# The last pass of a two-layer attention and MLP backward: the first dV chunk put ahead of delta, and dW operands in four row strips

## The chip, the cores and the metric

The kernel runs on one core of a Trainium2 chip. The metric is device time in microseconds of one execution, the median of several runs; lower is better. A profiled execution of the kernel before is read besides.

## The reference

Two residual layers, an attention block (A) and an MLP block (B), are applied twice with the same weights, to two tokens (batch 2, one position each). The outputs are the result and the gradients of nine inputs for a given `grad_out`. Cut to what matters:

```python
q = (x @ wq).reshape(B, 1, 32, 128)              # D = 1024, 32 query heads, 4 kv heads
scores = einsum("bhqd,bhkd->bhqk", q, k) * 128 ** -0.5   # 16384 cached keys
p = softmax(scores); o = einsum("bhqk,bhkd->bhqd", p, v)
A = o.reshape(B, 1, 4096) @ wo
B = gelu(layernorm(x) @ w1 + b1) @ w2 + b2       # F = 3584
x = x + A(layernorm(x)); x = x + B(layernorm(x)) # twice
grads = vjp(f)(grad_out)                         # dx, dK, dV, dWq, dWo, dW1, db1, dW2, db2
```

All tensors are bf16. K and V are 32 MB each, and so are dK and dV, which sum over both layers.

## The kernel before

Vectors live as columns: 128 partitions by (128-blocks x 2 tokens). Work runs in passes: layer 0 and layer 1 forward, then backward through layer 1, the second MLP, layer 0. A weight or cache tile (128 x 4096 bf16, 1 MB) comes in by SP's DMA queue; PE transposes its 128x128 blocks against an identity, ACT or DVE copies the result out of PSUM, and PE multiplies. Exponentials of both layers stay on chip (`e_all`).

**Evacuations.** `evac_bf16` (lines 150 to 156) and `evac_cast` (158 to 164) copy out of PSUM on ACT or on DVE, whichever has the smaller running cost in `load`; `only["e"] = "A"` forces ACT. The program order on each engine is the order of emission (a manual schedule).

**Before the last pass.** The backward of Wo for layer 0 is `wob`, an `Ahead`: its 32 row blocks are loaded and transposed in place by `wob.row` while the gradient is not yet there; every fifth (`dotted`: 4, 9, ... 29) is not transposed but done by DVE dot products (`wob.dots`, line 337). `wob.products` (line 379) makes dO. `do_delta` scales dO by the softmax's reciprocal sums (`dof`, 837 and 841), casts it to `doT_bf`, multiplies by o, sums over partitions on PE (`part_sum`, line 182) and writes the negated sums (delta) as three bf16 parts into `dlr` (849 to 861).

**The last pass** makes dV and dK of both layers at once, dQ of layer 0, and all weight gradients. A group `g` is one (batch, kv head); `order` runs through eight groups, each in four chunks of 4096 keys; `chunks[i]` is the i-th of the 32. For a chunk: `make_blks` (1197) transposes its coefficients (for dV: `e_all`; for dK: `dX`) into `blk`; `make_qm` (1165 to 1173) spreads the columns of dO or q into `Qm`; `kv_pair(w, i, h)` (1222) makes half a chunk of dV or dK with 8 matmuls into four PSUM banks and four copies, and after the second half stores the chunk (POOL's queue, line 1045). `scores` (1257) multiplies V by dO, `ds0` (1261, 1265) subtracts delta by a product with `dlr` and multiplies by `e_all` into `dX`; `dq_quad` (450) multiplies K by `dX`.

The first group is kept on chip (`keepV0` to `keepV3`, `keepK0` to `keepK3`) and is done ahead of the main loop: per chunk scores, `ds0`, and one `kv_pair`. Then the loop over steps `m` begins; a step takes two 8-block slices of V through transposes (line 1367), `scores`, at most one chunk's `make_blks`, `kv_pair`s, and with `step_fill` 1 unit (first four steps) or 5 units of weight-gradient work.

**Weight-gradient units.** dW = xT y over only four rows (two layers x two tokens). `rows_unit` (1012) transposes column vectors into rows: one source per 32-partition strip of `rowsA` and `rowsB`. A dW unit (1081) is one matmul, 4 x 128 by 4 x 512, into one of four banks and one copy; each weight gradient keeps to one strip (dW2 strip 0, dW1 strip 1, dWo strip 2, dWq strip 3). `fill` alternates dW2 and dW1 units, then dWo; `late` holds dWq of a kv head whose dq is done.

**Tiles and queues.** Staging tiles and load tiles are the same set: `new_home` takes a free tile for a store, `load_tile` one for a load (stored ones first, so the load waits for the store to land). `pump` issues loads while at most `NLD` are open and more than `spare` tiles are free. SP's queue and POOL's run in order. What the page calls L163 and L160 are the copies of `evac_cast`, L155 and L152 those of `evac_bf16`.

Of the kernel before, what the change touches and what calls it, by code (L numbers as in the profile page):

```python
# [9 lines left out]
BF16 = mybir.dt.bfloat16  # L10
# [13 lines left out]
def kernel(  # L24
# [155 lines left out]
    def part_sum(src, n, name):  # L180
        ps = pm_([128, n], F32, name)
        PE.matmul(ps[:], lhsT=onesf[:], rhs=src, start=True, stop=True)
        return ps
# [157 lines left out]
    class Ahead:  # L341


        def __init__(self, W, n_in, name, xT_bf=None, fps=None):
            self.W, self.J, self.x, self.fps, self.name = W, n_in // 128, xT_bf, fps, name
            self.dotted = range(4, self.J, 5)
            self.dp = vec.tile([128, len(self.dotted), 2], F32, name=name + "_dp")
            self.chunks = list(w_chunks(n_in, D))
            self.rows = {}
# [379 lines left out]
    n_all = vec.tile([128, DJ, 4], BF16, name="n_all")  # L729
    o_all = vec.tile([128, HQ, 4], BF16, name="o_all")  # L730
    dq_all = vec.tile([128, HQ, 4], BF16, name="dq_all")
    gA_all = vec.tile([128, DJ, 4], BF16, name="gA_all")
    m_all = vec.tile([128, DJ, 4], BF16, name="m_all")
    h_all = vec.tile([128, FJ, 4], BF16, name="h_all")
    dh_all = vec.tile([128, FJ, 4], BF16, name="dh_all")
    gM_all = vec.tile([128, DJ, 4], BF16, name="gM_all")
# [91 lines left out]
    def attn_out_bwd(l, gT):  # L828
        V.tensor_copy(out=gA_all[:, :, lsl(l)], in_=gT[:])
        _, dops = w_pass(A_wo, HD, D, "do_ps", gT_bf=gA_all[:, :, lsl(l)])  # L830
        return do_delta(l, dops)

    def do_delta(l, dops, ahead=None):
        sv = saved[f"a{l}"]
        dof = wrk.tile([128, G, 8], F32, name="dof")
        for b in range(2):
            V.tensor_tensor(out=dof[:, b * HKV:(b + 1) * HKV, :].rearrange("p k r -> p (k r)"), in0=dops[:, :, b],
                            in1=sv["rbc"][:, b * HKV:(b + 1) * HKV, :].rearrange("p k r -> p (k r)"), op=ALU.mult)
            if ahead is not None:
                r_ = sv["rbc"][:, b * HKV:(b + 1) * HKV, :].rearrange("p k r -> p (k r)")  # L840
                V.tensor_tensor(out=dof[:, b * HKV:(b + 1) * HKV, :].rearrange("p k r -> p (k r)")[:, 4:HQ:5],
                                in0=ahead.dp[:, :, b], in1=r_[:, 4:HQ:5], op=ALU.mult)
        doT_bf = vec.tile([128, G, 8], BF16, name=f"doT_bf{l}")
        V.tensor_copy(out=doT_bf[:], in_=dof[:])
        prod = wrk.tile([128, G, 8], F32, name="dprod")
        V.tensor_tensor(out=prod[:], in0=dof[:], in1=sv["oT"][:], op=ALU.mult)
        dlp = part_sum(prod[:].rearrange("p g r -> p (g r)"), G * 8, "dl_ps")
        rest_ = wrk.tile([128, G * 8], F32, name="dl_rest")
        V.tensor_scalar(out=rest_[:], in0=dlp[:], scalar1=-1.0, scalar2=None, op0=ALU.mult)
# [12 lines left out]
        saved[f"a{l}"]["doT_bf"] = doT_bf  # L862
        return doT_bf
# [94 lines left out]
    x4 = mlp_out(1, fps[:, 0:DJ * WIDE].rearrange("p (j b) -> p j b", b=WIDE)[:, :, 0:2])  # L958
    sv = saved["m0"]
# [33 lines left out]
    TP = [pt([128, 8, 128], BF16, "tpm%d" % i) for i in range(2)]  # L993
    for t in TP:
        V.memset(t[:].bitcast(F32), 0.0)
    do_delta(0, pairs(dops, HQ), wob)

    rowsA = ld.tile([128, LDW], BF16, name="rowsA", tag="ld")  # L1000
    rowsB = wrk.tile([128, D], BF16, name="rowsB", tag="rowout")

    def rows_unit(srcs, dst, j0):

        def u():
            tp = mtp()
            n = 0
            for i, (colT, jlo) in srcs.items():
                jn = min(8, colT.shape[1] - jlo)
                n = max(n, jn)  # L1010
                for j in range(jn):
                    PE.transpose(tp[32 * i:32 * i + 4, j, :], colT[:, jlo + j, :], ident[:], tile_position=(0, 32 * i))  # L1012
            lo, hi = 32 * min(srcs), 32 * max(srcs) + 4
            evac_bf16(dst[lo:hi, j0 * 128:(j0 + n) * 128], tp[lo:hi, 0:n, :].rearrange("p a b -> p (a b)"), n * 128)

        return Unit(u)

    X = [px([128, 512], F32, "xm%d" % i) for i in range(4)]
    rot = {"x": 0, "tp": 0}


    by_read = deque(ld.tile([128, LDW], BF16, name="big", tag="ld") for _ in range(NLD - 1))
    by_store = deque()

    def nxt(what, lst):
        rot[what] += 1
        return lst[(rot[what] - 1) % len(lst)]

    def mx():
        return nxt("x", X)  # L1030

    def mtp():
        return nxt("tp", TP)

    def n_free():
        return len(by_read) + len(by_store)

    def new_home():
        return (by_read or by_store).popleft()

    def load_tile():
        return (by_store or by_read).popleft()

    def store(out_ap, view, tile_):
        nc.gpsimd.dma_start(out_ap, view)  # L1045
        by_store.append(tile_)

    class Unit:
        def __init__(self, f, home=False):
            self.f, self.home = f, home  # L1050

        def ready(self):
            return not self.home or n_free() > 3

        def __call__(self):
            self.f()

    def dbias(rows, i, n, out_ap, name):
        p = 32 * i
        row = new_home()  # L1060
        for c0 in range(0, n, 512):
            ps = mx()
            PE.matmul(ps[p:p + 1, :], lhsT=ones_bf[p:p + 4, 0:1], rhs=rows[p:p + 4, c0:c0 + 512], start=True, stop=True,
                      tile_position=(p, p))
            evac_cast(row[p:p + 1, c0:c0 + 512], ps[p:p + 1, :], 512)
        store(out_ap.rearrange("(o f) -> o f", o=1), row[p:p + 1, 0:n], row)

    def dw_units(xrows, yrows, i, chunks, y0, ny, out_of):

        p = 32 * i  # L1070
        box = {}
        units = []
        for j0, rb in chunks:
            for j in range(rb):
                for c0 in range(0, ny, 512):
                    def u(j0=j0, rb=rb, j=j, c0=c0):
                        if j == 0 and c0 == 0:
                            box["t"] = new_home()
                        sv_ = box["t"][:, 0:rb * ny].rearrange("p (j n) -> p j n", j=rb)
                        ps = mx()  # L1080
                        PE.matmul(ps[:], lhsT=xrows[p:p + 4, (j0 + j) * 128:(j0 + j + 1) * 128],  # L1081
                                  rhs=yrows[p:p + 4, y0 + c0:y0 + c0 + 512], start=True, stop=True, tile_position=(p, 0))
                        evac_cast(sv_[:, j, c0:c0 + 512], ps[:], 512)
                        if j == rb - 1 and c0 + 512 >= ny:
                            store(out_of(j0, rb), sv_, box["t"])
                    units.append(Unit(u, j == 0 and c0 == 0))
        return units

    def rows_of(out_ap):
        return lambda j0, rb: out_ap[j0 * 128:(j0 + rb) * 128, :].rearrange("(j p) n -> p j n", p=128)  # L1090
# [45 lines left out]

    fill = deque()
    fill.append(rows_unit({0: (gM_all, 0), 1: (m_all, 0), 2: (gA_all, 0), 3: (n_all, 0)}, rowsB, 0))
    for j0 in range(0, HQ, 8):
        srcs = {0: (h_all, j0), 1: (dh_all, j0), 2: (o_all, j0)}  # L1140
        fill.append(rows_unit({i: v for i, v in srcs.items() if j0 < v[0].shape[1]}, rowsA, j0))
    units = [dw_units(rowsA, rowsB, 0, list(w_chunks(F, D)), 0, D, rows_of(out_8)),
            dw_units(rowsB, rowsA, 1, list(w_chunks(D, F)), 0, F, rows_of(out_6))]
    while any(units):
        for u_ in units:
            if u_:
                fill.append(u_.pop(0))
    fill.append(Unit(lambda: dbias(rowsB, 0, D, out_9, "db2"), True))
    fill.append(Unit(lambda: dbias(rowsA, 1, F, out_7, "db1"), True))
    fill.extend(dw_units(rowsA, rowsB, 2, list(w_chunks(HD, D)), 0, D, rows_of(out_5)))  # L1150
# [3 lines left out]

    cols = {}
    for w in "VK":
        cols[w] = vec.tile([128, G, 2, 8], BF16, name="cols" + w)
        for k in range(2):
            src = saved["a%d" % k]["qT_bf" if w == "K" else "doT_bf"]
            V.tensor_copy(out=cols[w][:, :, k, :], in_=src[:])  # L1160
# [70 lines left out]
    dq0 = vec.tile([128, G, 8], F32, name="dqT0")  # L1231
    dn0 = vec.tile([128, DJ, 2], F32, name="dn0")
    V.memset(dn0[:], 0.0)
# [9 lines left out]
    def quarter(kv):  # L1243

        quarters[kv][1]()
        late_pe.append(quarters[kv][3])
        late.append(rows_unit({3: (dq_all, kv * 8)}, rowsA, kv * 8))
        late.extend(dw_units(rowsB, rowsA, 3, [(0, 4), (4, 4)], kv * D, D,
                             lambda j0, rb: dwq_v[:, j0:j0 + rb, kv * D:(kv + 1) * D]))
# [66 lines left out]

    open_dq(order[0])
    qs = [make_qm(w, order[0]) for w in "VK"]
    for c in range(NCH):
# [100 lines left out]
```

## Time and profile before

| | before |
|---|---|
| median of 4 runs | 1163.57 us (1162.46 to 1165.48) |
| profiled execution | 1163.82 us, span 1162.0 us |
| busy: PE, DVE, ACT, POOL | 953.1, 639.5, 562.3, 63.9 us |
| TensorE clock granted (mean) | 0.832 |
| DMA | 449.30 MB, mean 387 GB/s |
| read, written | 348.14 MB, 98.58 MB |
| last pass, from the start of dO's scaling | 741.19 to 1162 us |

Times are microseconds from the start of the span; PEclk is the TensorE clock granted, 1.00 being full; a timeline row gives start, length, engine, line, operation, output and inputs, how many were merged (x), and in brackets the engine's idle time before it and what ended it. The ends of matmuls are modelled.

### The profile page before, as it was taken

The numbers are of one execution on the slowest core, as the hardware profiler recorded it, in microseconds if no ns is written. First come the engines' busy times: TensorE is split into PE (matmuls) and PEld (weight loads), VectorE is DVE, ScalarE is ACT, GpSimd is POOL, SyncE is SP. The second block draws the span as 40 slices with busy tenths as digits, with TensorE's granted clock in tenths as the row PEclk, the third lists the DMA queues.
The fourth block names the chain that finished last, engine by engine and source line by source line (L and its number), as shares of the span: only waits on it lengthen the run. The fifth ranks groups of instructions, "written<-read, shape, count | busy, mean of one in ns | idle before, by whom it ended". The sixth has DMA issues, their size and how long they took to land. (4 is left out here: it accounts for less than half of the span.)

```text
span 1162.0 us, 39945 instructions
## 1 busy us (share of the span) xinstructions
PE 953.1 (82%) x17565; PEld 729.7 (63%) x17565; DVE 639.5 (55%) x1344; ACT 562.3 (48%) x1410; POOL 63.9 (6%) x113
## 2 busy tenths in 40 slices
PE   4888895487879885899986799788998988998786
PEld 3867673387767765888765688555545554555452
DVE  1535351133545433454845355867777866787674
ACT  0534351022535430344454454457676866786673
POOL 0000000000000000000000000001111111111111
PEclk9989795597989875899998899788777977797785
DMA  9999999998999989999999899687999999999995
GB/s 370 418 419 419 419 418 397 396 370 351 418 419 418 418 322 418 381 356 401 380 415 410 326 363 353 250 302 305 400 421 423 417 421 421 420 419 420 424 417 230
DMA packets 89130, 449.30 MB, mean 387 GB/s; under 512 B 7026, under 2 KB 7026, under 8 KB 49788
## 3 DMA queue, kind: packets, MB, share of 16 engines
q1 hardware_dynamic: 72204, 348.17, 75.0%
q0 software_dynamic: 16752, 98.59, 20.5%
q8 instruction: 137, 2.24, 0.8%
q14 instruction: 37, 0.30, 0.1%
HBM read 348.14 MB, written 98.58 MB: 384 GB/s over the span
## 5 line engine op out<-in xcount | busy, mean ns | idle before, releaser
L152 ACT COPY kT<-tp 128x512 int32<-128x512 int32 x209 | 122.8, 587 | 256.0 <-PE tp L418 244.7
L155 DVE COPY kT<-tp 128x1024 bf16<-128x1024 bf16 x159 | 108.7, 690 | 109.7 <-PE tp L418 97.5
L418 PE MATMUL tp<-ident,kv_K 128*128 128x128 bf16 x1728 | 144.5, 232 | 5.2 <-DMA kv_K<-in_A_k_cache_dram 5.1
L418 PEld LDWEIGHTS <-kv_K 128*128 128x128 bf16 x1728 | 109.5, 104 | 6.2 <-DMA kv_K<-in_A_k_cache_dram 5.8
L163 DVE CAST big<-xm 128x512 bf16<-128x512 f32 (+1 forms) x138 | 89.9, 686 | 28.9 <-PE xm L1222 14.6
L160 ACT CAST big<-xm 128x512 bf16<-128x512 f32 (+1 forms) x159 | 86.8, 594 | 25.5 <-PE xm L1081 14.5
L571 PEld LDWEIGHTS <-kT 128*128 128x128 bf16 x2048 | 76.3, 98 | 28.1 <-issue 22.3
L571 PE MATMUL sc<-qT_bf,kT 128*128 128x8 bf16 x2048 | 92.0, 171 | 0.7 <-issue 0.6
L268 PE MATMUL wtp<-ident,wt 128*128 128x128 bf16 x928 | 76.5, 230 | 4.5 <-issue 3.2
L304 PEld LDWEIGHTS <-wt 128*128 128x128 bf16 x1696 | 49.0, 103 | 46.0 <-issue 14.7
L535 ACT ACTIVATE e_all<-sc,negm 128x64 bf16<-128x64 f32 x256 | 77.2, 345 | 1.1 <-DVE negm L530 1.0
L418 PE MATMUL tp<-ident,kv_V 128*128 128x128 bf16 x864 | 69.6, 227 | 9.7 <-DMA kv_V<-in_A_v_cache_dram 8.9
L163 DVE CAST keepK<-xm 128x512 bf16<-128x512 f32 x94 | 61.1, 685 | 16.0 <-PE xm L1222 12.7
L450 PE MATMUL acc_all<-kv_V,e_all 128*16 128x256 bf16 x864 | 46.4, 294 | 27.7 <-DMA kv_V<-in_A_v_cache_dram 15.7
L155 DVE COPY wT<-wtp 128x1024 bf16<-128x1024 bf16 (+1 forms) x65 | 41.5, 645 | 47.8 <-PE wtp L268 44.2
L152 ACT COPY wT<-wtp 128x512 int32<-128x512 int32 (+1 forms) x59 | 33.5, 568 | 68.8 <-PE wtp L268 59.3
L160 ACT CAST keepK<-xm 128x512 bf16<-128x512 f32 x103 | 55.4, 592 | 22.0 <-PE xm L1222 20.9
L160 ACT CAST keepV<-xm 128x512 bf16<-128x512 f32 (+1 forms) x91 | 49.4, 594 | 34.0 <-PE xm L1222 28.2
L163 DVE CAST keepV<-xm 128x512 bf16<-128x512 f32 (+1 forms) x81 | 52.8, 685 | 19.4 <-PE xm L1222 16.1
L418 PEld LDWEIGHTS <-kv_V 128*128 128x128 bf16 x864 | 55.2, 101 | 11.2 <-DMA kv_V<-in_A_v_cache_dram 9.7
L268 PEld LDWEIGHTS <-wt 128*128 128x128 bf16 x928 | 58.5, 103 | 5.1 <-issue 3.7
L535 ACT ACTIVATION_READ_ACCUMULATOR e_all<-sc,negm 128x1 f32 x256 | 60.2, 235 | 0.0
(344 smaller groups left out, 1772.5 us busy)
## 6 DMA issues: line engine op xcount, KB each, us to landing
kv_K<-in_A_k_cache_dram SPq DMA_DIRECT2D x81, 1024.0 KB, 12.7
kv_V<-in_A_v_cache_dram SPq DMA_DIRECT2D x81, 1024.0 KB, 12.7
out_dram<-big POOLq DMA_DIRECT2D x36, 1024.0 KB, 18.4
wt<-in_A_wo_dram SPq DMA_DIRECT2D x32, 1024.0 KB, 10.8
wt<-in_B_w_dram SPq DMA_DIRECT2D x32, 896.0 KB, 14.3
out_dram<-keepK POOLq DMA_DIRECT2D x22, 1024.0 KB, 17.7
out_dram<-keepV POOLq DMA_DIRECT2D x18, 1024.0 KB, 17.7
wt<-in_A_wq_dram SPq DMA_DIRECT2D x16, 1024.0 KB, 9.2
```

The lines of the kernel that those rows point to most:

```text
L152: S.copy(out=dst.bitcast(I32), in_=src.bitcast(I32))
L155: V.tensor_copy(out=dst, in_=src)
L160: S.copy(out=dst, in_=src)
L163: V.tensor_copy(out=dst, in_=src)
L268: PE.transpose(tp[:, o, :], wv[:, j, (o0 + o) * 128:(o0 + o + 1) * 128], ident[:])
L304: PE.matmul(fps[:, jo, :].rearrange("p (a b) -> p a b", b=2), lhsT=wv[:, j, jo * 128:(jo + 1) * 128], rhs=xT_bf[:, j0 + j, :].unsqueeze(1) ...
L418: PE.transpose(tp[:, j, :], cv[:, b * 8 + j, :], ident[:])
L450: PE.matmul(self.acc[cg:cg + 16, :], lhsT=coef(u), rhs=self.cv[:, t:t + 2, :].rearrange("p t d -> p (t d)"), start=False, stop=True, tile_ ...
L535: S.activation(out=e_all[:, g, f * half:(f + 1) * half, l, h, :], in_=sc[g][f][:, h, :].rearrange("p (a b) -> p a b", b=2), func=ACT.Exp, ...
L571: PE.matmul(sc[g][f][:, :, t % TH], lhsT=kT[:, j, :], rhs=q_bf[:, g, :], start=True, stop=True)
```

## The change

1. `do_delta` is split: `do_scaled` (scaling, cast straight into `cols["V"]`, product with o), `delta_mm` (PE's sum, into one of the four `xm` banks) and `delta` (the DVE chain). The first dV chunk's `kv_pair`s stand before anything that needs delta; the `scores` of chunks 1 and 0 go between, into the small bank and a transpose bank.
2. `make_blks(0)` and `make_blks(1)` are put directly behind the last `wob.products`, ahead of `do_scaled` on PE and DVE.
3. While the first chunk is made, all copies are ACT's (`only["e"] = "A"`); then DVE is charged 1.0.
4. `dotted` ends before 28: block 29 of Wo is transposed, not dotted.
5. Row operands: `R` has four regions; a vector is written as rows either the same in all four strips (`rows_rep`) or split over them (`rows_split`, `rows_by_512`), by transposes of 32 columns (columns beyond the four are zeros or neighbours). Consecutive dW units stand in different strips. `dw_units` runs over columns outside, blocks inside; `fill` alternates four dW2 with four dW1 units.
6. Two row units (`feed(2)`) stand ahead of the last two `dq_quad` pairs; the rows of gA and o are made after the biases, n's as the first `late` unit, dq's per kv head.
7. `colsV`, `colsK` (but dO of layer 0) and the zeroing of `dn0` move ahead of the W1 backward pass. The memsets of two transpose banks go; eight small memsets at the start of the kernel clear the ends of the column vectors.

```diff
-    def do_delta(l, dops, ahead=None):
+    def do_scaled(l, dops, dst, ahead=None):
...
-        V.tensor_copy(out=doT_bf[:], in_=dof[:])
+        V.tensor_copy(out=dst, in_=dof[:])
         V.tensor_tensor(out=prod[:], in0=dof[:], in1=sv["oT"][:], op=ALU.mult)
...
-            self.dotted = range(4, self.J, 5)
+            self.dotted = range(4, FJ, 5)
...
+    def rows(name, dst, at, n, j0=0, slots=8):
+        tp = mtp()
+        flat = whole[name][:].rearrange("p j b -> p (j b)")
+        for k in range(slots):
+            for i in range(4):
+                j = at(i, k)
+                if j is not None and j < n:
+                    j += j0
+                    PE.transpose(tp[32 * i:32 * i + 32, k, :], flat[:, 4 * j:4 * j + 32], ident[:],
+                                 tile_position=(0, 32 * i))
...
+    def rows_rep(name, dst, j0=0):
+        rows(name, dst, lambda i, k: k, 8, j0)
+    def rows_split(name, dst, n):
+        rows(name, dst, lambda i, k: 4 * k + i, n, 0, n // 4)
+    def rows_by_512(name, dst, n):
+        rows(name, dst, lambda i, k: 16 * (k // 4) + 4 * i + k % 4, n)
+    def dw_units(x, y, chunks, ny, out_of, split):
...
+            todo = [(j, c) for c in range(ny // 512) for j in range(rb)]
...
+                    if split == "x":
+                        p, xo, yo = 32 * (jj % 4), jj // 4 * 128, c * 512
+                    else:
+                        p, xo, yo = 32 * (c % 4), jj * 128, c // 4 * 512
+                    PE.matmul(ps[:], lhsT=x[p:p + 4, xo:xo + 128], rhs=y[p:p + 4, yo:yo + 512], start=True, stop=True,
+                              tile_position=(p, 0))
...
-    for t in TP:
-        V.memset(t[:].bitcast(F32), 0.0)
-    do_delta(0, pairs(dops, HQ), wob)
...
-        late.append(rows_unit({3: (dq_all, kv * 8)}, rowsA, kv * 8))
+        late.append(Unit(lambda: rows_rep("dq_all", dqr, kv * 8)))
...
-    open_dq(order[0])
-    qs = [make_qm(w, order[0]) for w in "VK"]
-    for c in range(NCH):
-        dp = mx()[:].rearrange("p (q t) -> p q t", t=TC)
-        for b in range(NB):
-            scores(c, b, kept_vT(c)[:, b * 8:(b + 1) * 8, :], dp)
-        ds0(c, dp)
...
+    make_blks(0, None)
+    make_blks(1, None)
+    open_dq(order[0])
+    prod = do_scaled(0, pairs(dops, HQ), cols["V"][:, :, 0, :], wob)
+    only["e"] = "A"
+    fix("x", [px([128, 512], F32, "xm%d" % i) for i in range(4)])
+    qv = make_qm("V", order[0])
+    dl_bank = mx()
+    delta_mm(prod, dl_bank)
+    open_dp = {}
...
+    kept_scores(1, sm_dp())
+    qv()
+    delta(0, dl_bank)
+    kv_pair("V", 0, 0)
+    kept_scores(0, pt([128, 16, TC], F32, "dp0")[:])
+    kv_pair("V", 0, 1)
+    ds0(0, open_dp[0])
+    fix("tp", [pt([128, 8, 128], BF16, "tpm%d" % i) for i in range(2)])
+    ds0(1, open_dp[1])
+    only["e"] = None
+    charge("D", 1.0)
+    kept_scores(2, sm_dp())
+    kv_pair("V", 1, 0)
+    ds0(2, open_dp[2])
+    for q in range(2):
+        dq_quad(0, q)
+    kept_scores(3, sm_dp())
+    kv_pair("V", 1, 1)
+    ds0(3, open_dp[3])
+    qs = make_qm("K", order[0])
+    for q in range(2):
+        dq_quad(1, q)
+    qs()
+    feed(2)
+    for c in (2, 3):
+        for q in range(2):
+            dq_quad(c, q)
```

## The prediction

> **What bounds the kernel now.** I read first the windows by stage, then the timelines of the engines, of POOL and of SP where the last pass begins, then the timeline of its tail. The stages (columns: stretch in us, length, busy us and instructions of each engine, granted TensorE clock, share and rate of the DMA engines):
>
> ```profile
> core 0: us, PE busy (x) PEld busy (x) DVE busy (x) ACT busy (x) POOL busy (x), PEclk, DMA share, GB/s
> 738.00:746.00 8.00, 1.71 (x22) 1.23 (x23) 6.66 (x29) 0.15 (x1) 0.00 (x0) 0.72 0.85 351
> 746.00:762.00 16.00, 13.91 (x237) 7.53 (x233) 8.18 (x15) 5.28 (x10) 0.58 (x1) 0.50 0.23 78
> 762.00:784.00 22.00, 18.23 (x341) 13.97 (x338) 15.82 (x27) 14.13 (x28) 2.14 (x4) 1.00 0.88 336
> 784.00:806.00 22.00, 18.91 (x259) 11.63 (x259) 16.81 (x28) 16.37 (x32) 2.13 (x4) 0.84 0.68 269
> 806.00:1115.00 309.00, 272.31 (x3561) 163.09 (x3560) 235.43 (x398) 220.54 (x424) 46.68 (x78) 0.79 1.02 419
> 1138.00:1152.00 14.00, 11.73 (x104) 5.00 (x101) 7.74 (x15) 7.74 (x14) 1.83 (x3) 0.50 0.46 184
> ```
>
> From 806 to 1115 the DMA engines are full at 419 GB/s: a faster engine buys nothing there. They are not full before (78 GB/s from 746 to 762, 269 from 784 to 806) nor at the end (184). So the change can pay in two places, the way into that plateau and the tail. The way in:
>
> ```profile
> 736.91 1.24 ACT L152 COPY wt<-turn 128x512 int32<-128x512 int32 x2 [0.22 <-PE turn L320]
> 740.07 0.08 DVE L337 DVE_READ_ACCUMULATOR junk<-wt,wob_g 128x1 f32 x1
> 740.26 1.03 DVE L995 MEMSET tpm<- 128x512 f32 x2
> 741.19 0.17 DVE L837 TENSOR_TENSOR dof<-wob_b,rbc 128x32 f32<-128x32 f32 x1
> 755.81 0.58 POOL L1045 DMA_DIRECT2D out_dram<-keepV  x1 [46.19 <-ACT keepV L160]
> 762.01 1.07 PE L1367 MATMUL tpm<-ident,keepxV 128*128 128x128 bf16 x16
> ```
>
> PE ends dO at 738.57, DVE its dots at 740.15, the memsets follow, dO begins at 741.19, the first store leaves at 755.81, and step 0 of the main loop begins at 762.01. SP's queue shows why nothing is read meanwhile: its first load after 737.76 goes into the tile that this store frees.
>
> ```profile
> 760.12 0.33 SPq L1119 DMA_DIRECT2D keepV<-in_A_k_cache_dram  x1
> 767.60 0.33 SPq L1119 DMA_DIRECT2D keepV<-in_A_v_cache_dram  x1
> ```
>
> From 762 to 806 the waits name PE, DVE and ACT only, never a DMA: steps 0 to 7 run at the engines' own pace (PE 86%, DVE 76%, ACT 74% busy from 784), and the DMA engines drain to nothing (0.21 busy from 795 to 800). So **a store or load that leaves earlier pays nothing by itself; what pays is how much earlier step 8 (its first copy is at 812.15) begins.** The tail:
>
> ```profile
> 1137.74 1.01 PE L1012 MATMUL tpm<-ident,dq_all 128*4 128x128 bf16 x8 [0.61 <-DVE dq_all L894]
> 1146.28 5.27 PE L1081 MATMUL xm<-rowsA,rowsB 4*128 4x512 bf16 x12 [0.49 <-ACT keepK L160]
> 1151.59 0.59 ACT L160 CAST big<-xm 128x512 bf16<-128x512 f32 x1 [0.21 <-PE xm L1081]
> ```
>
> Twelve dWq matmuls in one strip go 0.42 us apart; their copies (0.59 on ACT, 0.69 on DVE) could leave one each 0.32.
>
> **The change part by part.** The sum is made against the profiled execution: 1163.82 us, span 1162.0, so 1.8 around it; it lies 0.25 above the median 1163.57. About 0.2%, 2.3 us, is what a measurement of this kernel can tell from no change.
>
> *Start of the kernel.* Eight memsets stand on DVE before the first layernorm; small ones there are 0.06 each, 0.5 us. PE's first pass over Wq then waits for loads again and again (2.77 us at 18.18, then 1.47 each), so they are hidden: 0. Were that cover gone, 0.5.
>
> *Before the W1 pass.* Three copies (0.13 each, half of the 0.26 rows of two) and one memset (0.07) move ahead of its first evacuation, which DVE takes at 697.11; PE had waited for it and waits for nothing long afterwards: +0.46 (0 to 0.46).
>
> *Row 29 of Wo by PE and ACT instead of DVE.* DVE loses two dots of 1.27. ACT, which sets the pace there (copies 0.59 long, 0.62 apart), gets one copy, but the gap of 0.26 that a dotted row left goes: +0.5 (0.35 to 0.65). PE ends at 738.57 + 0.46 + 0.5 = 739.55, DVE's dots well before.
>
> *Ahead of dO on DVE.* The two memsets go (0.93 up to dO's start). In come two coefficient-block copies (0.41 each) that wait for transposes just behind the last product, and the accumulator's memset (0.27): 739.55 + 0.3 + 0.82 + 0.27 = 740.95, against 741.19: −0.25.
>
> *First dV chunk.* colsV is ready 0.9 later, at 741.85; before it was ready at 745.2, behind delta's chain (743.02 to 745.1). PE then does the transpose (0.28), delta's product (0.69), 32 scores (1.03) and the selection (0.4, ready after 0.7); ACT copies QmV (0.38): the first pair's matmuls begin at 744.8. Delta's DVE chain runs beside this and ends before its reader. ACT alone copies eight halves, 0.535 each, starting 0.68 after a pair's first matmul, with 0.55 between pairs: 744.8 + 0.68 + 2.14 + 0.55 + 2.14 = 750.3. First store 750.6: 5.2 earlier.
>
> *Chunks 1 to 3.* Now serial through one score bank: dX of chunk 1 ends at 750.25, scores 1.05, pair 0.68, two copies on each engine 1.29, dX 0.69: 754.0. Again 1.05 + 0.68 + 1.29: second store 757.35, 4.9 earlier. dX of chunk 3, r16 and QmK's selection bring PE to 758.4. Behind them wait two row units on PE, 60 transposes; the old 32 at 764.35 took 1.22, 0.04 each: 2.4. Then chunks 2 and 3 of dQ (1.9): **step 0 at 762.7, +0.7, but with 2.4 us of row work already done.**
>
> *Steps 0 to 7.* Before, five row units there cost PE 1.22 + 1.0 + 1.0 + 1.0 + 0.5 = 4.7; now 8 + 32 + 28 transposes, 0.4 + 1.3 + 1.15 = 2.85: −1.85. dW units: 19 before, two strips in turn, 0.2 each; 21 now, in fours over four strips, 0.13 each: −1.1. Copies hardly change (−0.15 per engine). If copies alone set the pace, −0.15; if PE does, −2.95. PE is the busiest, so I take all of the rows and a bit over half of the dW: −2.5. Step 8: 0.7 − 2.5 = **−1.8 us** (bounds −2.3 and +0.55).
>
> *Loads and stores in order.* By step 8 the code has issued as many loads and stores as before. The K load that it issued at the end of step 3 comes at step 7, behind the seventh store; its data are used in step 11 (830 before), and K loads into these tiles took 9.8 to land: 0. The plateau then carries the same bytes and moves with step 8. The new units there (rows of gA and o) are covered by the full DMA engines.
>
> *Tail.* The dq rows are 32 transposes instead of 8; at half clock 8 took 1.01. If 32 go four at a time it is the same, at 0.04 each 0.5 more: +0.3. The first four dW matmuls gain 0.1, since the product behind them waits for the first copy's bank. The last twelve become bound by copies: 12 × 0.32 + one bank turn = 4.0 against 5.27: −1.3. Sum **−1.1 us** (bounds −2.2, +0.3).
>
> A rule that speaks against the strips: the Trainium skill, TensorEngine Tiling (Array Packing), section PSUM Bottleneck, says that tiling speeds TensorE but not the emptying of PSUM. By the fourfold speedup of its overview alone the twelve matmuls would fall to about 1.3 us (an estimate), and the whole to about 1158.2. The copies' rows above agree with the rule, and the sum goes by them.
>
> Sum: 1163.8 − 1.8 − 1.1 = **1160.9**, I say 1160.8.
>
> **The rivals.**
>
> *No shift of step 8.* Copies set the pace of steps 0 to 7 and the entry stays at +0.7: +0.55 there, −1.1 in the tail: 1163.2. For it: DVE and ACT wait for PE only by short stretches between pairs. Against: PE is busier than both. Within 0.2%.
>
> *Row transposes go one after another: slower.* The operands are now 32 columns wide, not 4. If that keeps them from overlapping, they cost what eight cost at half clock, 0.105 each, or about 0.055 at full clock. Place: 60 before step 0 (6.3 instead of 2.4, +3.9), 60 in steps 1 and 2 (+0.9), 32 in the tail (3.4 instead of 1.3, +2.1): 1160.8 + 6.9 = 1167.7. It decides from about 0.07 each. For it: in the tail's row even 4-column ones went 0.105 apart, in one strip. Against: 32 over four strips went 0.04 apart at 764.35.
>
> *The clock stays up.* The row from 746 to 762 has it at 0.50; PE had stood idle from 738.57 to 742.29. Now that gap is about 1.3 us, cut by the block transposes. At full clock pairs take 0.40 instead of 0.61, dlr's product 0.38 instead of 0.59, dQ's eight 0.40 instead of 0.57: four, four and eight of them, about 3 us in all: 1157.8. Against it: PE still waits for copies between the pairs.
>
> The Trainium skill, TensorE: Matmul & The Clock Gate, section What's actually happening, says that about 3.4 us of idling halve the clock and about 3.4 us of busy work restore it; the first agrees with the 3.72 us gap in the trace, and by the rule the full clock would be kept and the time be 1157.8.
>
> **How the numbers follow.** Forecast 0.45, no shift 0.22, clock up 0.12, serial transposes 0.21. Of the forecast 0.05 and of the no-shift case 0.20 lie within 0.2%, 0.02 of the latter above. Faster 0.40 + 0.12 = 0.52; same 0.25; slower 0.21 + 0.02 = 0.23. Range: the forecast's low ends (−2.3, −2.2) give 1159.3, the clock case with the 0.46 of the W1 pass back and a little more in the tail 1157.0; the high ends (+0.55, +0.3) give 1164.7, and 1165.2 takes in the edge of the serial case.
>
> **What would show it.** Right: first store near 750.6, second near 757.4, step 0 near 762.7, step 8 (812.15 before) near 810.3, plateau still 419 GB/s and as long, tail from the dq rows to the last dW copy 1.1 shorter (14.4 before). Wrong: step 0 after 765 or transposes over 0.07 apart; a DMA among the waits of steps 4 to 8; a plateau below 415 GB/s, since everything here assumes that only its start moves.

## The result, and the profile after

The changed kernel takes 1169.52 us (median of 43 runs, 1165.52 to 1175.08), the kernel before 1165.61 us on the same chips (62 runs, 1161.0 to 1172.44): ratio 1.0034, 95% interval 1.0025 to 1.0042. It is slower, by some 4 us; the forecast was 1160.8. That was summed from 1163.57, the median of the first four runs of before, so 2 of the 8.7 us between forecast and result lie in the base. The profiled execution of after took 1167.84 us, span 1165.4, so 1.7 less than its median.

The stages of after, with the columns of the windows shown of before:

```profile
core 0: us, PE busy (x) PEld busy (x) DVE busy (x) ACT busy (x) POOL busy (x), PEclk, DMA share, GB/s
738.00:746.00 8.00, 5.92 (x140) 5.31 (x137) 5.63 (x22) 3.40 (x7) 0.00 (x0) 1.00 1.01 418
746.00:762.00 16.00, 11.12 (x195) 6.08 (x198) 8.86 (x18) 4.32 (x9) 1.12 (x2) 0.51 0.49 192
762.00:784.00 22.00, 18.69 (x362) 13.85 (x351) 14.11 (x25) 13.59 (x28) 1.19 (x3) 0.89 0.70 280
784.00:806.00 22.00, 18.36 (x228) 10.73 (x228) 16.78 (x29) 15.44 (x30) 2.01 (x4) 0.73 0.62 238
806.00:1115.00 309.00, 266.72 (x3632) 159.69 (x3630) 233.35 (x395) 218.68 (x418) 47.07 (x79) 0.78 1.01 413
1138.00:1152.00 14.00, 9.64 (x140) 5.36 (x141) 7.68 (x16) 6.54 (x13) 1.07 (x2) 0.50 0.53 219
```

The gap behind dO is filled (192 GB/s from 746 to 762, 78 before), but the 44 us behind it have become worse: 280 and 238 GB/s against 336 and 269, and the granted clock is 0.89 and 0.73 against 1.00 and 0.84. (dO starts 2.06 us later here; with windows moved by as much it is 265 and 233 GB/s, 0.94 and 0.69.) The way in, from the timelines of the engines, of POOL and of SP's queue:

```profile
743.25 0.18 DVE L849 TENSOR_TENSOR dof<-wob_b,rbc 128x32 f32<-128x32 f32 x1
746.76 2.05 ACT L160 CAST keepV<-xm 128x512 bf16<-128x512 f32 x4 [0.54 <-PE xm L1259]
749.29 2.05 ACT L160 CAST keepV<-xm 128x512 bf16<-128x512 f32 x4 [0.48 <-PE xm L1259]
751.65 0.58 POOL L1002 DMA_DIRECT2D out_dram<-keepV  x1 [39.08 <-ACT keepV L160]
753.01 2.48 DVE L163 CAST keepV<-xm 128x512 bf16<-128x512 f32 x4 [1.71 <-PE xm L1259]
757.74 2.48 DVE L163 CAST keepV<-xm 128x512 bf16<-128x512 f32 x4 [1.64 <-PE xm L1259]
760.52 0.54 POOL L1002 DMA_DIRECT2D out_dram<-keepV  x1 [8.28 <-DVE keepV L163]
761.29 1.04 PE L1026 MATMUL tpm<-ident,gM_all 128*32 128x128 bf16 x32
762.12 0.96 PE L1026 MATMUL tpm<-ident,h_all 128*32 128x128 bf16 x28
762.87 1.92 PE L450 MATMUL acc_all<-keepK,keepV 128*16 128x256 bf16 x32
764.72 1.89 PE L1428 MATMUL tpm<-ident,keepxV 128*128 128x128 bf16 x16
799.09 0.33 SPq L1177 DMA_DIRECT2D big<-in_A_k_cache_dram  x1
```

From here on, times "from dO" are counted from the first `dof` instruction (741.19 before, 743.25 here). The first store leaves at 8.4 from dO (14.6 before). But all eight copies of chunk 1 stand on DVE, 2.48 for four; step 0 begins at 21.47 (20.82 before), at half clock (16 transposes 1.89, before 1.07); and the K load that before issued at 781.38 comes at 799.09. The tail:

```profile
1142.66 1.04 PE L1026 MATMUL tpm<-ident,dq_all 128*32 128x128 bf16 x32 [0.62 <-DVE dq_all L911]
1150.79 4.07 PE L1061 MATMUL xm<-dqr,nr 4*128 4x512 bf16 x12 [0.49 <-ACT keepV L160]
1152.66 2.82 ACT L160 CAST keepxV<-xm 128x512 bf16<-128x512 f32 x5 [0.18 <-PE xm L1061]
```

From the dq rows to the last dW copy it is 12.8 us (1142.66 to 1155.48), 14.4 before: 1.6 shorter, where the forecast had 1.1.

### The profile page after: what moved, and what is told of

It is laid out like the page before. It is cut to its first block, busy times and chain, and to the rows that moved or that the text cites. A ratio compares the mean times of both kernels' runs of the same rounds, so it can differ in the third digit from the quotient of the medians.

```text
span 1165.4 us, 40316 instructions
## 1 busy us (share of the span) xinstructions
PE 955.2 (82%) x17749; PEld 732.1 (63%) x17749; DVE 636.4 (55%) x1348; ACT 562.6 (48%) x1411; POOL 63.9 (5%) x113
## 5 line engine op out<-in xcount | busy, mean ns | idle before, releaser
L418 PE MATMUL tp<-ident,kv_K 128*128 128x128 bf16 x1728 | 147.3, 236 | 3.4 <-DMA kv_K<-in_A_k_cache_dram 3.4
L418 PEld LDWEIGHTS <-kv_K 128*128 128x128 bf16 x1728 | 111.9, 105 | 4.0 <-DMA kv_K<-in_A_k_cache_dram 3.8
L163 DVE CAST big<-xm 128x512 bf16<-128x512 f32 (+1 forms) x123 | 79.8, 685 | 25.0 <-PE xm L1061 10.8
L160 ACT CAST big<-xm 128x512 bf16<-128x512 f32 x140 | 76.1, 593 | 21.6 <-PE xm L1259 10.9
L304 PEld LDWEIGHTS <-wt 128*128 128x128 bf16 x1696 | 48.9, 103 | 46.5 <-issue 14.8
L163 DVE CAST keepK<-xm 128x512 bf16<-128x512 f32 x98 | 63.6, 684 | 20.8 <-PE xm L1259 15.1
L160 ACT CAST keepK<-xm 128x512 bf16<-128x512 f32 x115 | 62.4, 593 | 23.8 <-PE xm L1259 14.6
L160 ACT CAST keepV<-xm 128x512 bf16<-128x512 f32 (+1 forms) x108 | 57.9, 592 | 27.2 <-PE xm L1259 23.4
L163 DVE CAST keepV<-xm 128x512 bf16<-128x512 f32 (+1 forms) x90 | 58.4, 684 | 19.6 <-PE xm L1259 14.9
L1061 PE MATMUL xm<-rows 4*128 4x512 bf16 x176 | 49.7, 413 | 14.9 <-ACT keepV L160 2.6
## 6 DMA issues: line engine op xcount, KB each, us to landing
wt<-in_A_wo_dram SPq DMA_DIRECT2D x32, 1024.0 KB, 11.4
wt<-in_B_w_dram SPq DMA_DIRECT2D x32, 896.0 KB, 14.4
out_dram<-keepK POOLq DMA_DIRECT2D x24, 1024.0 KB, 17.7
```

The lines of the kernel that those rows point to most:

```text
L160: S.copy(out=dst, in_=src)
L163: V.tensor_copy(out=dst, in_=src)
L304: PE.matmul(fps[:, jo, :].rearrange("p (a b) -> p a b", b=2), lhsT=wv[:, j, jo * 128:(jo + 1) * 128], rhs=xT_bf[:, j0 + j, :].unsqueeze(1) ...
L418: PE.transpose(tp[:, j, :], cv[:, b * 8 + j, :], ident[:])
L1061: PE.matmul(ps[:], lhsT=x[p:p + 4, xo:xo + 128], rhs=y[p:p + 4, yo:yo + 512], start=True, stop=True, tile_position=(p, 0))
```

## The experiments

Each kernel was timed in 12 runs (the one with fillers on after in 6) beside 23 to 35 runs of the kernel before on the same chip; ratios are to that. The first theories were four. **Theory 1**: the K load that comes 18 us later starves the DMA engines. **Theory 2**: the way into the main loop costs (one-sided copies, half clock at step 0). **Theory 3**: the strips themselves cost. **Theory 4**: the longer column vectors or the moved tiles slow the forward part; in the profile of after the second MLP's hidden gradient is already 2.7 us later, ahead of all that the change moves but the memsets. Two more came out of the first four kernels. **Theory 5**: TensorE's clock is at half for longer in steps 5 to 9. **Theory 6**: that comes of the row units put ahead of step 0.

### The halves of the change

The new order with the old row and dW units (`a_order`; it keeps the old column vectors, and zeroes the two transpose banks behind the first chunk's delta):

```diff
-    R = ld.tile([128, LDW], BF16, name="rows", tag="ld")[:].rearrange("p (r n) -> r p n", r=4)
+    rowsA = ld.tile([128, LDW], BF16, name="rowsA", tag="ld")
+    rowsB = wrk.tile([128, D], BF16, name="rowsB", tag="rowout")
...
-    feed(2)
```

> The new order of the last pass's beginning (parts 1 to 3, 4 and 7 of the change) with the old row units and old dW units; no row unit stands ahead of the main loop, the column vectors keep their old layout, and the two transpose banks are zeroed by DVE behind the first chunk's delta. The K load of the fifth group's first chunk is issued at the end of step 3 again. Theory 1 (the late K load loses the time): about the time of before, ratio 0.998 to 1.001. Theory 2 (the way into the main loop loses it: all eight copies of chunk 1 on DVE, half clock at step 0): slower, 1.002 to 1.004, with step 0 more than 2 us later than in before by the start of dO's scaling. Theory 3 (the strips themselves cost): 0.998. Theory 4 (the new layout of the column vectors slows the forward part): 0.998 to 1.000.

Measured: 1167.09 us, ratio 1.0027 (1.0009 to 1.0046).

The strips on the old order (`b_strips`):

```diff
-    rowsA = ld.tile([128, LDW], BF16, name="rowsA", tag="ld")
+    R = ld.tile([128, LDW], BF16, name="rows", tag="ld")[:].rearrange("p (r n) -> r p n", r=4)
...
-    fill.append(rows_unit({0: (gM_all, 0), 1: (m_all, 0), 2: (gA_all, 0), 3: (n_all, 0)}, rowsB, 0))
+    fill.append(Unit(lambda: rows_rep("gM_all", R[0])))
...
```

> Before with part 5 alone: row operands in four strips, dW units in fours over the strips, the longer column vectors with their eight memsets; old order of the last pass's beginning. The first dW unit falls in step 4, so the K load is issued at the end of step 3 as in before. Theory 1 (late K load): faster by the tail and the saved transposes, 0.997 to 0.999. Theory 2 (way into the main loop): the same, 0.997 to 0.999. Theory 3 (the strips cost): 1.002 to 1.004. Theory 4 (the layout slows the forward part by about 2 us): 1.000 to 1.002, with dO's scaling 2 us later than in before.

Measured: 1163.57 us, ratio 0.9978 (0.9962 to 0.9994). The strips gain 2 to 3 us, so theory 3 falls. About 1 us of this is the two memsets ahead of dO (1.03 on DVE), which the strips make needless and `b_strips` leaves out: from the hidden gradient to dO it takes 43.6 us, before 44.7. The order loses some 3. Both together should be near 1.0005; after has 1.0034, so there is a third loss, in something that neither half has. The two row units ahead of step 0 are such a thing.

### What it is not

The K load issued in step 3 again, in after (`c_load`):

```diff
-    Unit.spare = 3
+    Unit.spare = 4
...
+        if m == NCH:
+            Unit.spare = 3
         step_fill(1 if m < NCH else 5)
```

> After with one thing changed: up to step 3 a dW unit takes a staging tile only if more than four are free, so that none is taken in step 3 and the K load of the fifth group's first chunk is issued at the end of step 3 as in before, 18 us earlier. Theory 1 (this load's delay starves the DMA engines, 1.1 MB or 2.6 us): about 1167, ratio 1.0005 to 1.0015 against before, the cumulative DMA bytes at step 12 level with before. Theories 2, 3 and 4: no change from after, 1.003 to 1.004.

Measured: 1169.76 us, ratio 1.0033 (1.0014 to 1.0052), the same as after, with the load at 38.6 from dO (55.8 in after). Theory 1, my first, falls.

The longer column vectors and their memsets alone on before (`f_cols4`), and parts 4 and 7 alone on before (`j_moved`):

```diff
-    n_all = vec.tile([128, DJ, 4], BF16, name="n_all")
+    n_all = cols4(DJ, "n_all")
...
```

> Before with only the longer column vectors and their eight memsets at the kernel's start. Theory 4 (they shift the tiles in SBUF or hold up the start): slower by 1 to 2 us, 1.001 to 1.002, and the mlp's hidden gradient 2 to 3 us later in the profile. Theories 1 to 3, and the prediction (0 for the memsets): no change, 0.9993 to 1.0007.

```diff
-            self.dotted = range(4, self.J, 5)
+            self.dotted = range(4, FJ, 5)
...
+            if w + str(k) != "V0":
+                V.tensor_copy(out=cols[w][:, :, k, :], in_=saved["a%d" % k]["qT_bf" if w == "K" else "doT_bf"][:])
...
```

> Before with parts 4 and 7 of the change alone: block 29 of Wo transposed instead of dotted, the copies into colsV and colsK (but dO of layer 0) and the zeroing of dn0 ahead of the W1 backward pass, with their tiles allocated there. Order of work up to the W1 pass is that of before to the instruction. By the prediction's terms: 0.46 + 0.5 to the last product of dO, less what leaves the stretch behind dO: 0 to +1 us, 1.000 to 1.001. If the other places of the tiles slow the forward part (the three profiles of the new order had the mlp's hidden gradient 2.7 to 3.7 us later than before, the other old-order ones 0.8): 1.002 to 1.003. If that was chance: the hidden gradient within 2 us of 697.9, the mean of the four profiles of the old order.

Measured: 0.9997 (0.9976 to 1.0018) and 1.0002 (0.9986 to 1.0018). The profile of the second has the hidden gradient at 700.29, 3.8 later than in before's profile, and yet the time does not differ: what the forward part does in a single profile was chance. Thirteen of the kernels, after among them, run the same instructions on PE, DVE and ACT up to there, and their profiles have it anywhere from 697.27 to 701.69. Theory 4 falls, as far as intervals of some 2 us to each side can tell.

### The one-sided copies

After, with the running costs reset where ACT's turn ends (`d_bal`):

```diff
-    charge("D", 1.0)
+    load["A"] = load["D"] = 0.0
```

> After with the running costs of the two copying engines set to zero where the first chunk's copies end, in place of DVE's charge of 1.0: the eight copies of chunk 1 are then shared by ACT and DVE instead of all falling on DVE. Theory 2 (these copies lose the time): each pair's copies take 1.3 us instead of 2.48, step 0 begins 2 us earlier by dO's start and the time falls by 2 to 4 us, ratio 1.000 to 1.002. Theory 5 (the TensorE clock at half speed in steps 5 to 9 loses it): step 0 begins up to 2 us earlier but the time changes by under 2 us, 1.002 to 1.004.

Measured: 1166.2 us, ratio 1.0007 (0.9992 to 1.0022). Its timelines:

```profile
754.86 1.07 ACT L160 CAST keepV<-xm 128x512 bf16<-128x512 f32 x2 [1.60 <-PE xm L1259]
754.96 1.29 DVE L163 CAST keepV<-xm 128x512 bf16<-128x512 f32 x2 [1.75 <-PE xm L1259]
760.35 0.54 POOL L1002 DMA_DIRECT2D out_dram<-keepV  x1 [6.20 <-ACT keepV L160]
```

Two copies on each engine, as the prediction had assumed; the second store leaves at 15.5 from dO instead of 17.3, and the first `kT` copy of step 0 comes at 18.1 instead of 22.5. Why DVE had them all is plain in the code: while `only` forces ACT, ACT's cost grows with each copy, and DVE is charged only 1.0 afterwards. Theory 2 holds for this part.

### The row units ahead of step 0

After without them (`g_nofeed`), and with both repairs (`k_dg`):

```diff
-    feed(2)
```

> After without the two row units ahead of the last dQ products: the four row units fall in steps 0 to 4 as in the kernel with the strips alone, and the first dW unit in step 4. Additive theory (order alone +2.9, strips alone -2.1 by the means): about +0.8, ratio 1.0007. Theory 6 (the row units ahead of step 0 are what makes the two parts worse together): 1.000 to 1.001, step 0 some 1.8 us earlier by dO's start. Theory 5 (half clock in steps 5 to 9, whatever the units' place): 1.003 to 1.004, with more than 10 us at half clock between 40 and 76 us after dO's start.

> After with both repairs: the copies of chunk 1 shared by the two engines, and no row units ahead of the last dQ products. Theory 2 and 6 together (each cause costs its own 2.8 us): 1166.9 - 2.8 in means, ratio 0.998 to 0.999, step 0 at 16 to 17 us from dO's start. If both repairs mend the same loss: 1.0005 to 1.001.

Measured: 1166.44 us, 1.0008 (0.9987 to 1.0029); and 1161.16 us, **0.9975** (0.9961 to 0.9988), faster than both kernels. The other way round, the strips on the old order with two row units ahead (`n_bfeed`), and after with both repairs of copies and load and the row units moved up into waits (`q_gap`):

```diff
         if c == 1:
             kv_pair("V", 1, 1)
+            for _ in range(2):
+                fill.popleft()()
```

> The strips alone on the old order, with two row units put ahead of the last dQ products as in after. Theory 6 (row units there run at half clock, and leave PE's work thin in steps 2 to 4, so that the clock falls in steps 4 to 9): slower than the strips alone by 2 to 3 us, ratio 1.000 to 1.001, 10 us or more at half clock between 40 and 68 us from dO's start. If the place of the rows is harmless: 0.997 to 0.999.

```diff
+    load["A"] = load["D"] = 0.0
+    feed(1)
     kept_scores(2, sm_dp())
...
+    feed(1)
     kept_scores(3, sm_dp())
...
-    feed(2)
...
```

> After with the copies of chunk 1 shared, the K load at the end of step 3, and the two early row units moved up into waits: one ahead of the scores of chunk 2, one ahead of those of chunk 3, where PE waits for copies of the first two chunks. If rows ahead of step 0 cost only by the time they take there: step 0 at 16 to 17.5 us from dO's start, 0.997 to 0.999. Theory 6 (thin work in steps 2 to 4 lets the clock fall): step 0 as early, but a long spell at half clock in steps 4 to 9, and 1.000 to 1.002.

Measured: 1165.8 us, 1.0008 (0.9995 to 1.0022), and 1165.33 us, 1.0000 (0.9982 to 1.0018). Three pairs that differ by the row units ahead (after and `g_nofeed`; `n_bfeed` and `b_strips`; `q_gap` or `d_bal` and `k_dg`) all give them a price of 0.25 to 0.32%, some 3 us, each uncertain by about 0.2%. Another rival stands in these pairs: with the row units ahead the first dW unit comes sooner, and the K load then leaves late (55.8 from dO in after, 37.2 in `g_nofeed`; 56.3 and 39.9; 51.4 in `d_bal`, 37.5 in `k_dg`). But it leaves early in both kernels of `q_gap` and `k_dg` (36.0, 37.5) and of `c_load` and `g_nofeed` (38.6, 37.2), and these pairs give 0.25% too. In `q_gap` the row units delay nothing: its first `kT` copy comes at 17.0 from dO, in `k_dg` at 17.7. So there the loss lies behind step 0. In after itself step 0 also comes 2.8 us later than in `g_nofeed` (22.5 and 19.7), so a part of its price may stand ahead. One profile of each, in us:

| kernel | row units | ratio | at half clock, 36 to 68 from dO | step 0 to 4 | step 0 to 14 | step 0 to the end |
|---|---|---|---|---|---|---|
| before | in steps | 1 | 6.8 | 21.9 | 90.6 | 399.3 |
| `b_strips` | in steps | 0.9978 | 6.8 | 20.3 | 90.0 | 397.1 |
| `g_nofeed` | in steps | 1.0008 | 7.5 | 20.0 | 89.7 | 397.5 |
| `k_dg` | in steps | 0.9975 | 9.9 | 20.3 | 89.8 | 398.5 |
| after | ahead | 1.0034 | 13.7 | 20.5 | 92.5 | 399.6 |
| `n_bfeed` | ahead | 1.0008 | 10.2 | 21.4 | 89.5 | 401.4 |
| `c_load` | ahead | 1.0033 | 23.9 | 21.1 | 95.5 | 403.9 |
| `d_bal` | ahead | 1.0007 | 23.9 | 20.2 | 95.8 | 401.1 |
| `q_gap` | ahead | 1.0000 | 14.2 | 21.6 | 96.1 | 403.3 |

(Half-clock time is worked out from windows of 2 us as twice the sum of length times one minus PEclk; steps are counted between first `kT` copies.) Two things stand in it. Steps 0 to 4 take as long with two row units more in them as without: there they fill waits, so taking them out gains nothing. And with the row units ahead, PE is at half clock longer between 36 and 68 us from dO, which is steps 4 to 7 or so. Single profiles don't all fit: `n_bfeed` loses its time only behind step 14, and `a_order` and `j_moved`, with the old row units in the steps, had 10.2 and 13.7 us at half clock and 94.6 and 94.5 from step 0 to 14, and `j_moved` is no slower than before. So a long spell in one profile does not tell that a kernel is slow. The spells vary from run to run; the last column and the ratios count, and the cause wanted a test of its own.

One number is on record for every run, the granted clock averaged over the whole execution. Its means over the runs are lower with the row units ahead: 0.821 in `d_bal` and in `q_gap` against 0.827 in `k_dg`, and 0.824 in `n_bfeed` against 0.829 in `b_strips`, each known to 0.001 to 0.002. Only after and `g_nofeed` (0.822 and 0.823) don't differ by more than that. It speaks for the clock, but does not say in which steps.

### Whether the clock is the cause

Fillers that nobody reads, on after (102) and on the strips alone (256), `h_warm` and `i_bwarm`:

```diff
+    def warm(n):
+        t = warm_bank()
+        for j in range(n):
+            PE.transpose(t[:, j % 8, :], ident[:], ident[:])
...
+                    if 3 <= m < 10:
+                        warm(6)
                     kv_pair(w, at[m_ - h], h)
```

> After with six filler transposes of the identity ahead of every pair of steps 3 to 9, into a transpose bank that the next real transposes overwrite; nothing reads them. Theory 5 (the clock falls to half there since PE's work is too thin between the waits for banks): the clock stays at 1.00 through most of 40 to 76 us after dO's start, the stretch from step 0 to step 14 takes about 90 us instead of 92.5, and the ratio falls to 1.000 to 1.002. If the clock has no part in it: the fillers cost some 0.1 to 0.3 us a step, 1.004 to 1.006.

> The strips alone on the old order, with filler transposes of the identity: 56 while dO is scaled, 32 during delta's chain, 12 ahead of the scores of chunks 1 to 3 of the kept group, 6 ahead of each pair up to step 9. Theory 5: the clock, at 0.5 from the end of dO's products to step 0 in before, stays at 1.00 for most of that stretch and of steps 5 to 9; step 0 begins 2 to 3 us earlier by dO's start and the time falls to 1159 to 1161 in medians where before is 1164.6, ratio 0.995 to 0.997. If the fillers only add PE work: 0.998 to 1.000.

Measured: 1172.75 us, 1.0056 (1.0035 to 1.0076), and 1169.81 us, 1.0035 (1.002 to 1.005). The clock did as expected; in the first one, in windows of 8 us from 36 from dO:

```profile
core 0: us, PE busy (x) PEld busy (x) DVE busy (x) ACT busy (x) POOL busy (x), PEclk, DMA share, GB/s
782.43:790.43 8.00, 6.19 (x101) 3.98 (x97) 5.19 (x10) 4.88 (x9) 0.53 (x1) 1.00 0.61 248
790.43:798.43 8.00, 6.36 (x96) 3.98 (x89) 6.46 (x11) 6.22 (x13) 1.06 (x2) 1.00 0.41 166
798.43:806.43 8.00, 5.97 (x98) 3.64 (x96) 5.65 (x9) 5.94 (x12) 0.53 (x1) 1.00 0.77 289
```

But steps 0 to 8 took 53.1 us instead of 50.0. Of the 102 fillers 78 stand there, in 13 groups of six that take at least 0.43 each to the next instruction, 5.6 us (an estimate): net of them 47.5 remain. Both times missed what theory 5 had led me to expect: 1.0056 is where the first expectation put it if the clock had no part in the loss, and 1.0035 is worse than either of its cases. Taken alone they speak against the theory. My reading is that the fillers, which stood ahead of every pair, in the path, cost more than the clock gave; these two runs do not show that. The cleaner test sets fillers only where the row units had been. `e_both` is after with shared copies and the early load, row units ahead; `s_again` adds to it the 60 transposes of these units once more, unread:

```diff
+        if m in (3, 4):
+            again("gM_all" if m == 3 else "h_all", 32 if m == 3 else 28)
         step_fill(1 if m < NCH else 5)
```

> After with the copies of chunk 1 shared and the K load at the end of step 3 again; the two row units stay ahead of the last dQ products. If the late load costs anything once step 0 comes early: faster than with the shared copies alone (1.0007), 0.998 to 0.999. Theory 6 (the row units ahead cost by the clock in steps 4 to 9): 1.000 to 1.0015, step 0 near 18 us from dO's start, over 10 us at half clock between 36 and 68 us, and 92 us or more from step 0 to step 14 against 90 of the kernels with row units in the steps.

> As the kernel before it, with the 60 transposes of those two row units made once more, unread, at the end of steps 3 and 4. Theory 6: the clock stays up as in the kernels with row units in the steps (about 7 us at half clock between 36 and 68 us from dO's start), step 0 to step 14 takes 90 to 91 us, and the added work pays for itself: 0.998 to 0.9995. If the loss has another cause: the added 2 us of PE work come on top, 1.001 to 1.003.

Measured: 1167.94 us, 1.0024 (1.0007 to 1.0041), against 1164.33 us, **0.9986** (0.9969 to 1.0002). Work that serves nothing makes the kernel some 4 us faster than `e_both`. (`e_both` is the slowest of three kernels with shared copies and row units ahead; against the mean of it, `d_bal` and `q_gap`, 1.0010, it is 2.8 us.) The mean clock over the 12 runs goes the same way, 0.822 and 0.826. The early load again gained nothing. PE's timeline shows how, first in `e_both` (steps 3 to 5):

```profile
780.56 0.40 PE L450 MATMUL acc_all<-keepxK,dX 128*16 128x256 bf16 x8
780.78 0.22 PE L1202 MATMUL tpm<-ident,colsV 128*16 128x128 bf16 x1
781.68 0.22 PE L1202 MATMUL tpm<-ident,colsK 128*16 128x128 bf16 x1 [0.69 <-ACT blk L152]
...
785.12 1.03 PE L1428 MATMUL tpm<-ident,big 128*128 128x128 bf16 x8
...
786.59 1.06 PE L320 MATMUL tpm<-ident,big 128*128 128x128 bf16 x8
...
793.04 1.03 PE L1428 MATMUL tpm<-ident,big 128*128 128x128 bf16 x8
```

and at the same place in `s_again`:

```profile
782.27 0.40 PE L450 MATMUL acc_all<-keepxK,dX 128*16 128x256 bf16 x8
782.49 0.62 PE L1390 MATMUL tpm<-ident,gM_all 128*32 128x128 bf16 x32
782.94 0.22 PE L1202 MATMUL tpm<-ident,colsV 128*16 128x128 bf16 x1
783.41 0.22 PE L1202 MATMUL tpm<-ident,colsK 128*16 128x128 bf16 x1 [0.26 <-ACT blk L152]
...
786.65 0.62 PE L1439 MATMUL tpm<-ident,big 128*128 128x128 bf16 x8
...
787.52 0.61 PE L320 MATMUL tpm<-ident,big 128*128 128x128 bf16 x8
...
792.93 1.03 PE L1439 MATMUL tpm<-ident,big 128*128 128x128 bf16 x8
```

The 32 transposes (0.45 to the next instruction) go into a wait of 0.69 for `blk` and leave 0.26 of it: they delay nothing. With them the same eight transposes of step 4 take 0.62, without them 1.03, and so do the next eight: from `colsK` to the first transposes of step 5 it is 9.5 us here, 11.4 there. The windows give the 3.41 us behind the moment at which the clock comes back to full (36.8 and 36.7 from dO), and the stretch from 44 to 60, `e_both` first:

```profile
780.31:783.72 3.41, 2.06 (x39) 1.44 (x39) 2.92 (x7) 2.04 (x5) 0.00 (x0) 1.00 1.02 423
787.54:795.54 8.00, 5.74 (x59) 3.01 (x58) 4.21 (x9) 5.00 (x10) 0.53 (x1) 0.50 0.67 267
795.54:803.54 8.00, 7.76 (x77) 4.17 (x76) 5.22 (x9) 5.30 (x10) 0.53 (x1) 0.50 0.32 132
```

```profile
782.00:785.41 3.41, 2.49 (x71) 1.88 (x72) 2.91 (x7) 2.03 (x5) 0.00 (x0) 1.00 1.02 358
789.31:797.31 8.00, 6.18 (x92) 3.77 (x92) 5.17 (x10) 4.97 (x10) 0.53 (x1) 0.68 0.64 262
797.31:805.31 8.00, 7.66 (x98) 4.91 (x95) 6.32 (x11) 5.47 (x11) 1.07 (x2) 0.71 0.34 133
```

The first lines of the two differ by the 32 transposes, 2.49 us of busy PE against 2.06. Behind them the clock falls at once in `e_both` (at 783.72, for 23.9 us), and in `s_again` it stays at 1.00 until 792.24. Half-clock time from 36 to 68 falls from 24.6 to 11.6 us, steps 0 to 8 from 53.7 to 50.9. PE's waits between steps 4 and 8 are alike (4.0 and 4.7 us): what differs is how long the same instructions take. For this pair theories 5 and 6 hold, though the clock came up by less than expected (11.6 us at half against about 7, 93.0 from step 0 to 14 against 90 to 91). That the row units cost by the clock in the other pairs too is inferred from it; no run there has the clock changed and nothing else.

## Why the prediction was wrong

**The step that failed** is "Steps 0 to 7: −2.5". From the first copy of step 0 to that of step 8 after takes 50.0 us, before 49.5: +0.6, and 52.1 to 53.7 in `c_load`, `d_bal` and `e_both`; with the strips and the row units in the steps, `b_strips`, it takes 48.9, −0.6. I took PE at 86% busy for a bound by the amount of PE's work, and the row transposes taken out of it for a gain. They had stood in waits (steps 0 to 4 take no longer with two units more in them); without them PE's work is thinner and, as `e_both` and `s_again` show, the clock falls. The row units ahead cost 3 us by three pairs of kernels, instead of gaining 1.85.

**A second term was mis-sized**: "two copies on each engine 1.29" in chunk 1. It was 2.48, all on DVE; the repair is worth 3 us by two pairs (after and `d_bal`, `g_nofeed` and `k_dg`), 1 by a third (`c_load` and `e_both`). That step 0 came at 21.47 from dO, where the working had 21.75, is luck, errors that met: the copies were late by some 2.4, but the first store left 1.25 sooner from dO than worked out (8.4 against 9.65), and PE's work ahead of step 0 was shorter (60 row transposes 1.6 us to the next instruction, not 2.4).

**What held.** Memsets, W1 pass and row 29: no cost that the times show (0.9997, 1.0002); from the hidden gradient to dO's start after takes 44.09 us, before 44.71. Loads and stores in order: 0, which I doubted first and wrongly (`c_load`). Tail: −1.5 from step 55's first copy to the end (44.1 to 42.6), −1.1 said: the 32 transposes take 1.04, what 8 took (1.01), so the +0.3 for them falls away, and the last twelve matmuls take 4.07, 4.0 said. The plateau fell short a little: from step 8 to step 55 it takes 307.0 us at 417 GB/s, before 305.7 at 419. (In the fixed window from 806 it is 413, under the 415 that was named as a sign of being wrong; but step 8 starts 3.7 us later there.)

**Two small slips of the working.** That the waits from 762 to 806 never name a DMA holds for PE, DVE and ACT; one wait of 7.1 us on POOL's queue ends with a K load. And 738.57 + 0.46 + 0.5 is 739.53, not 739.55. The result hangs on neither.

**The rivals.** Serial transposes: refuted, 32 in 1.04 at half clock. Clock up: it stayed at 1.00 only until about 746.4 (0.61 from 746 to 748, 0.50 behind). It fell as the first pair began (746.27), behind a wait of 1.77 us for `colsV` and one of 0.46 for `QmV`; so it was not the waits for copies between the pairs, which the prediction had against it. "No shift of step 8" named the right place; its mechanism, copies as the pace, was not what was found, and it had no loss in it.

**Open.** What an earlier step 0 is worth. `k_dg` has step 8 4.8 us earlier from dO than `b_strips`, and the two ratios (0.9975 and 0.9978) don't tell them apart. Of the price of after, some 4 us, 3 + 3 − 2.5 by copies, row units and strips is near enough; that the profile pair shows only +0.7 us from the hidden gradient to the end (466.24 against 465.52) shows how little one profile of each says here: `c_load`, with the same time as after, has 470.94.

## What to carry to other kernels

Ask of work that you move off a busy engine whether it stood in a wait: there it was free, and here it also kept the clock up; a busy share of 86% with waits of 0.7 us between is no proof that less work is faster. Where copies are forced to one engine and a running cost chooses afterwards, work out who gets the next ones. And where the effects are a few us, let ratios of kernels that differ by one edit carry the verdict, and profiles only the mechanism.

## What the runs showed of the hardware

In `e_both` the clock falls to half at about 784 (1.00 from 781.54 to 783.54, 0.50 from 787.54 on), though PE has waited no more than 0.77 us at a time in the 10 us ahead and was busy for 5.7 of the 8 us up to 783.5; it stays there for some 24 us, though PE works nearly without a pause from 796.8 to 808.9. The Trainium skill, TensorE: Matmul & The Clock Gate, section HAM oscillation — how this bites in real kernels, gives as the rule that PE should have no idle gaps over about 3.4 us. Here the clock fell with gaps a quarter as long; the measurement decides. How much work is enough the runs do not settle: at this place 2.06 us of busy PE in 3.41 let it fall and 2.49 kept it. Transposes of 32 columns in four strips, 32 of them, take 0.45 us to the next instruction at full clock (`s_again`) and 0.83 at half (761.29 to 762.12 in after), and in `s_again` they delayed nothing where they stood in a wait.
